# First entry's float32 attention scores on 64 rows of TensorE per head, with the first weight chunks issued by ScalarE

## The chip, the cores and the metric

One core of one Trainium2 chip runs the kernel. The metric is device microseconds of one execution. All times below are microseconds unless they are marked ns. The engines are called PE (TensorE, matrix products), DVE (VectorE), ACT (ScalarE), POOL (GpSimd) and SP (SyncE, which does no arithmetic here and issues transfers).

## The reference

Block-causal attention, followed by two feed-forward networks, all in float32:

```python
scores = scale * np.matmul(q, k.transpose(0, 1, 3, 2))      # (4, 8, 576, 576), head size 64
scores = np.where(block_i >= block_j, scores, -1000000000.0) # blocks of 64 positions
attn = softmax(scores); x = np.matmul(attn, v)               # x becomes (2304, 512)
h = np.maximum(np.maximum(x @ w1, x @ w2), x @ w3)           # d_ff 768
x = h @ w_out
h = np.maximum(x @ w_in, 0.0)                                # d_ff 2048
out = h * h @ w_out2
```

The scores of q and k are large enough that the kernel computes them in float32 or in a split form of it. The weights arrive as 8-byte numbers and are turned into a high and a low float32r part on the chip.

## The kernel before, in words

The batch has 4 entries; an entry has 8 heads, taken as 4 pairs, so there are 16 pairs. A pair's 576 query positions are cut into a first group of 256 (steps 0 and 1, of 128 each) and a second of 320 (steps 2 and 3, and a last step of 64). A step computes scores (tiles `sc`, in PSUM), masks a 64-wide corner, takes the row maximum (`nm`), exponentiates on ACT (`P`, with row sums `sm`), transposes P on PE (`tp`), copies it to SBUF (`ta`, `tb`) and, once per group, multiplies with v (`av`), scales by the reciprocal sums spread over rows (`r`, `rs`) and splits the result into `xh` and `xl`.

The first entry (pairs 0 to 3) takes its scores directly in float32. `score_operands_f32` (L486) loads three tiles: k of both heads on 128 partitions, and for each head a copy of q in which the other head's 64 partitions hold zeros. So each product contracts over 128 partitions, half of which add zero. In steps 0 and 1 the two heads' scores stand side by side in one PSUM bank, and one memset and one reduce serve both. The later entries split q and k into high and low parts and are not touched by the change, except that a small tile `zt` comes from an array of its own.

The weights of the first feed-forward network come in 24 chunks: 18 of `w1` (6 columns c, 3 matrices i, named `raw_w_c_i`) and 6 of `wo1`. A chunk is a transfer of 512 KB, two passes of ACT (128x512 each), two operations of DVE, an integer addition on POOL, a cast on ACT (`w1h`) and a subtraction on DVE (`w1l`). `with_weights` (L751) hands out the next chunk while it walks through the attention of the first entry: 0.7 chunks per step in the first groups of all four pairs, then 1.5 chunks per step in the second groups. The products `l` of the first feed-forward network (`mlp1`) need `xh`, `xl`, `w1h` and `w1l`; they share the PSUM banks with tag `mlp` with some of the score tiles, and come behind those.

The order on each engine isn't the order in which the program writes the operations. `Plan` collects them with their dependences and `Plan.issue` puts them out one by one: always the operation that by its own estimate can start first, on ties the one with the lower rank and then the one noted first. `duration` and `transfer` hold its prices. What it has put out each engine executes strictly in that order, so an instruction that waits holds up all behind it.

Eight completion semaphores are shared by the transfers in turn, so a transfer issued while eight are out waits until the oldest has landed.

Of the kernel before, what the change touches and what calls it, by code (L numbers as in the profile page):

```python
# [12 lines left out]
F32 = mybir.dt.float32  # L13
# [30 lines left out]

CFG = dict(PD=-1, PE=1, A1=0, A2=0, WP=1, FC=(8, 16), WO=55, FI=0, LO2=0, HI2=0, Q2=0, RN=3, XL=2, HL=2, SO=0, TF=0, W_A=0.7, W_B=1.5, SPARE='hl..rhl..rhl..r..r..r', S=15, PB=3, QB=(2, 2, 3), BANKS=(3, 2, 1, 2), LO=0, HI=0, Q=0, EV=('*', '*'), EV2=('a', 'a'), CB=2, PC=0, PM=1000, PX=-0.5, PO=0, HH='*', XH='*', N0='a', YS='a', HIS=0, RB=1, TB=(2, 1), KB=1, CT='a', LT='d', XA=4, XB=0)
W_A, W_B = CFG["W_A"], CFG["W_B"]
SPARE = CFG["SPARE"]
BANKS = dict(zip(("sc", "tp", "av", "mlp"), CFG["BANKS"]))

S_F32 = [CFG["S"] >> n & 1 for n in range(PAIRS)]  # L50
PB = CFG["PB"]
# [117 lines left out]
class Plan:  # L169
# [56 lines left out]
    def issue(self):  # L226
# [21 lines left out]
        for _ in ops:  # L248
            best = None
            for e, w in waiting.items():  # L250
                if not w:
                    continue
                other = held["pool" if e == "dve" else "dve"] if e in held else 0.0
                start = {i: max(free[e], at, other if port else 0.0) for i, (at, port) in w.items()}
                t = min(start.values())
                i = min((i for i, s in start.items() if s <= t), key=lambda i: (ops[i].rank, i))
                if best is None or t < best[0]:
                    best = t, e, i
            t, e, i = best
            op = ops[i]  # L260
            op.engine = e
            length = duration(e, op) * SLOW[e]
            if e in held and waiting[e][i][1]:
                held[e] = t + length - HOLD[e]
            for other in op.engines:
                del waiting[other][i]
            if e == "sp":
                queue = max(t + 1500, queue) + transfer(op)
                op.end, free[e] = queue + 400, t + 60
            else:  # L270
                op.end = t + length
# [41 lines left out]
def duration(engine, op):  # L313
# [3 lines left out]
    if engine == "pe":  # L317
        stat, mov = op.args[1:] if op.args[1:] else (op.kw["lhsT"], op.kw["rhs"])
        if op.name == "transpose":
            return 109  # L320
        n, m = width(op.args[0]), width(stat)
        if stat.tile.args[1] == F32:
            return (4 * n / 2.4 + 5) * (0.5 if m == 64 else 1)
        return max(n, 230) / 2.4 + (11 if n < 300 else 13)
# [17 lines left out]
def transfer(op):  # L342
    x = next(v for v in op.views())
    return 128 * 4 * width(x) / 320.0


@with_exitstack
def fused_kernel(ctx: ExitStack, tc: tile.TileContext, z0, k0, qk, v, w123, wo1, win2, wo2, out):
    nc = Plan(tc)
    mm = nc.tensor.matmul  # L350

# [6 lines left out]
    warm = const.tile([128, 1], F32, name="warm")  # L358
    tc.nc.vector.memset(warm, 0.0)
    tc.nc.scalar.activation(out=warm, in_=warm, func=AF.Exp)  # L360
    make_identity(tc.nc, ident.tile.real)
# [8 lines left out]
    at = Pool(nc, es_a.enter_context(tc.tile_pool(name="at", bufs=1, side="right", reuse_waits="tile")))  # L370
    ps = Pool(nc, ctx.enter_context(tc.tile_pool(name="ps", bufs=1, space=PSUM)), psum=True)

    def bank(name, tag):
# [7 lines left out]
    def load_w_(src, hi, lo, name, f=None):  # L381
# [8 lines left out]
        else:  # L390
            raw = m1.tile([128, 512, 2], U32, tag="wraw", bufs=2, name=f"raw_{name}")
            if f is None:
                f = m1.tile([128, 512], F32, tag="wf", bufs=2, name=f"f_{name}")
        nc.sync.dma_start(out=raw, in_=src.bitcast(U32).rearrange("p (n t) -> p n t", t=2))
        low, high = raw[:, :, 0], raw[:, :, 1]
# [59 lines left out]
    def score_operands(n):  # L455
# [18 lines left out]
        nc.sync.dma_start(out=kt, in_=k0[n])  # L474
        nc.sync.dma_start(out=zt, in_=z0[n, :, :, TAIL:])
        if CFG["TF"]:
# [9 lines left out]
    def score_operands_f32(n, g):  # L486


        a, w = GROUPS[g] if n < NPAIR else (0, S)
        if n < NPAIR and g == 0:  # L490
            zk = at.tile([128, 3, GA], F32, tag="tb", bufs=2 * CFG["TB"][1], name=f"zk{n}")
            z, k = [zk[:, h] for h in range(2)], zk[:, 2]
        else:
            z = [at.tile([128, w], F32, tag=t, bufs=CFG["QB"][2 * (t == "kl")], name=f"z{n}_{t}") for t in ("qs", "kl")]
            k = at.tile([128, S], F32, tag="kh", bufs=CFG["QB"][1], name=f"k{n}")
        nc.sync.dma_start(out=z[0], in_=z0[n, :, 0, a:a + w])
        nc.sync.dma_start(out=k, in_=k0[n, :, :a + w])
        nc.sync.dma_start(out=z[1], in_=z0[n, :, 1, a:a + w])
        return [[(z[h], k)] for h in range(2)], None

# [16 lines left out]
    def prefetch(n, g):  # L517


        f32 = bool(n < NPAIR and g == 0 or S_F32[n])  # L520
        with nc.ranked(CFG["PO"]):
            ops[n] = f32, score_operands_f32(n, g) if f32 else score_operands(n), value_operands(n, g)

    def attn_pair(n, groups=(0, 1)):
# [29 lines left out]
        def step(i):  # L554
# [3 lines left out]
            share = i < 2  # L558
            sc = [bank(f"sc{name}_{h}", sc_tag(i)) for h in range(1 if share else 2)]
            P = [at.tile([128, 576], F32, tag="P", bufs=PB, name=f"P{name}_{h}") for h in range(len(sc))]  # L560
            if share:
                both = sc[0][:, :2 * N].rearrange("p (h k) -> p h k", h=2)
                sc = [both[:, h] for h in range(2)]
                P = [P[0][:, N * h:N * h + N] for h in range(2)]
            nm = small(f"nm{name}")
            scale = SCALE if sf else 1.0
            sm = sums[i // 2][:, 2 * (i % 2):2 * (i % 2) + 2] if direct else small(f"sm{name}")
            for h in range(2):
                for c, (qp, kp) in enumerate(score[h]):
                    mm(sc[h][:, :N], qp[:, 128 * i - q0:128 * i - q0 + 128], kp[:, :N], start=c == 0,  # L570
                       stop=c == len(score[h]) - 1)
                if not share:
                    nc.vector.memset(sc[h][0:64, N - 64:N], MASKED / scale)
                    nc.vector.tensor_reduce(out=nm[:, h:h + 1], in_=sc[h][:, :N], axis=AX.X, op=ALU.max, negate=True)
            if share:
                nc.vector.memset(both[0:64, :, N - 64:N], MASKED / scale)
                nc.vector.tensor_reduce(out=nm, in_=both, axis=AX.X, op=ALU.max, negate=True)
# [173 lines left out]
    def with_weights(steps, per_step):  # L751
        due = 0.0
        for _ in steps:
            due += per_step
            while due >= 1:
                due -= 1
                f = next(weights, None)
                if f:
                    f()

    with_weights(attention(0, groups=(0,)), W_A)
    with_weights(attention(0, groups=(1,)), W_B)
# [286 lines left out]
```

## Time and profile before

| | us |
|---|---|
| runs | 884.64, 886.14, 887.04 (median 886.14) |
| the profiled execution | 888.7 |
| its span from first to last instruction | 886.9 |
| PE busy | 864.2 (97%) |
| DVE busy | 601.1 (68%) |
| ACT busy | 424.9 (48%) |
| POOL busy | 104.0 (12%) |

The profiled execution is longer than its span by 1.8, and 2.56 above the median of the runs. Shares over the whole span hide that the first 108 us are another kernel than the rest: there the weights are split and attention runs on ACT and DVE, and the transfers are dense. The trace is therefore read by stretches. All of the kernel's own operations carry one line, that of the helper which calls the engine (L187 before, L185 after), so groups are told apart by tile names.

### The profile page before, as it was taken

The numbers are of one execution on the slowest core, as the hardware profiler recorded it, in microseconds if no ns is written. First come the engines' busy times: TensorE is split into PE (matmuls) and PEld (weight loads), VectorE is DVE, ScalarE is ACT, GpSimd is POOL, SyncE is SP. The second block draws the span as 40 slices with busy tenths as digits, with TensorE's granted clock in tenths as the row PEclk, the third lists the DMA queues.
The fourth block names the chain that finished last, engine by engine and source line by source line (L and its number), as shares of the span: only waits on it lengthen the run. The fifth ranks groups of instructions, "written<-read, shape, count | busy, mean of one in ns | idle before, by whom it ended". The sixth has DMA issues, their size and how long they took to land.

```text
span 886.9 us, 14852 instructions
## 1 busy us (share of the span) xinstructions
PE 864.2 (97%) x5464; PEld 777.7 (88%) x5464; DVE 601.1 (68%) x1376; ACT 424.9 (48%) x1016; POOL 104.0 (12%) x94
## 2 busy tenths in 40 slices
PE   5899999999999999999999989999999999999997
PEld 4567799998999989899999979898999989999896
DVE  6998678878788988646557766546755457544543
ACT  6888667667688787544555231113211114211111
POOL 2233200000001111214442230000000000000000
PEclk9999999999999999999999999999999999999999
DMA  8745432232255563554656578454765536655221
GB/s 294 237 138 174 131 114 89 85 115 86 85 184 177 175 213 118 196 190 165 257 203 237 164 299 338 160 230 168 270 229 184 207 145 229 215 200 196 72 72 71
DMA packets 52056, 157.73 MB, mean 178 GB/s; under 512 B 8592, under 2 KB 16016, under 8 KB 48400
## 3 DMA queue, kind: packets, MB, share of 16 engines
q1 hardware_dynamic: 51984, 156.78, 50.5%
q8 instruction: 43, 0.70, 0.3%
q14 instruction: 29, 0.24, 0.1%
HBM read 124.26 MB, written 32.51 MB: 177 GB/s over the span
## 4 chain that ended last, share of the span: by engine, by line
PE 92%; DVE 2%; DMA 2%; ACT 2%; issue 0%; POOL 0%; SPq 0%; ACTq 0%; POOLq 0%; DVEq 0%
PE l L187 34%; PE acc L187 22%; PE ph_x L187 11%; PE ph_y L187 8%; PE av L187 5%; PE sc L187 5%; PE tp L187 4%; PE sc_t L187 2%; DMA raw_wi<-in_win 1%; PE tp_t L187 1%; DMA raw_wo<-in_wo 1%; DMA zk<-in_k 1%; PE r L187 0%; ACT P L187 0%; DVE f_wo L187 0%
## 5 line engine op out<-in xcount | busy, mean ns | idle before, releaser
L187 PE MATMUL acc<-woh,g 128*128 128x512 f32 x576 | 198.5, 395 | 0.0
L187 PE MATMUL l<-xh,w1l 128*128 128x256 f32 (+1 forms) x576 | 174.3, 303 | 0.9 <-DVE run L187 0.9
L187 PE MATMUL l<-xl,w1h 128*128 128x256 f32 (+1 forms) x576 | 172.2, 299 | 0.0
L187 PE MATMUL l<-xh,w1h 128*128 128x256 f32 (+1 forms) x576 | 172.2, 299 | 0.0
L187 ACT CAST g<-c 128x384 fp32r<-128x384 f32 x96 | 49.3, 513 | 220.8 <-DVE c L187 220.8
L187 PEld LDWEIGHTS acc<-woh,g 128*128 128x128 f32 x576 | 108.5, 189 | 19.4
L187 PE MATMUL acc<-wol,g 128*128 128x512 f32 x288 | 113.3, 393 | 0.0
L187 PEld LDWEIGHTS l<-xh,w1l 128*128 128x128 f32 x576 | 109.0, 189 | 4.1 <-issue 1.5
L187 PEld LDWEIGHTS l<-xl,w1h 128*128 128x128 f32 x576 | 109.1, 189 | 2.6 <-issue 1.7
L187 PEld LDWEIGHTS l<-xh,w1h 128*128 128x128 f32 x576 | 109.1, 189 | 1.9 <-issue 1.2
L187 PE MATMUL ph_x<-t,wq 128*128 128x384 f32 x432 | 87.7, 337 | 2.7 <-ACT p L187 2.7
L187 PEld LDWEIGHTS ph_x<-t,wq 128*128 128x128 f32 x432 | 77.4, 188 | 8.9 <-ACT p L187 3.1
L187 DVE TENSOR_TENSOR g<-c,g 128x384 fp32r<-128x384 f32 x96 | 53.6, 560 | 43.0 <-ACT g L187 42.6
L187 ACT ACTIVATE P<-sc,nm 128x128 f32<-128x128 f32 (+3 forms) x128 | 66.9, 530 | 9.9 <-DVE nm L187 8.4
L187 DVE TENSOR_TENSOR run<-l,run 128x256 f32<-128x256 f32 (+1 forms) x96 | 43.7, 455 | 27.9 <-PE l L187 26.3
L187 POOL TENSOR_TENSOR f_wo<-f_wo,raw_wo 128x512 int32<-128x512 int32 x22 | 29.8, 1357 | 276.5 <-DVE sm L187 180.3
L187 PEld LDWEIGHTS acc<-wol,g 128*128 128x128 f32 x288 | 54.3, 189 | 7.8
L187 PE MATMUL l<-hh,wo1l 128*128 128x256 f32 (+1 forms) x192 | 57.7, 306 | 2.2 <-DVE wo1l L187 2.1
L187 PE MATMUL ph_y<-b,wq 128*128 128x384 f32 x288 | 58.3, 337 | 0.0
L187 PE MATMUL l<-hl,wo1h 128*128 128x256 f32 (+1 forms) x192 | 57.5, 301 | 0.0
L187 PE MATMUL l<-hh,wo1h 128*128 128x256 f32 (+1 forms) x192 | 57.4, 300 | 0.0
L187 DVE TENSOR_REDUCE nm<-sc 128x2 f32<-128x256 f32 (+2 forms) x96 | 55.1, 588 | 0.8
(135 smaller groups left out, 1613.1 us busy)
## 6 DMA issues: line engine op xcount, KB each, us to landing
wq<-wq_d SPq DMA_DIRECT2D x20, 1792.0 KB, 8.6
wq_d<-wq SPq DMA_DIRECT2D x8, 1792.0 KB, 7.7
raw<-in_qk SPq DMA_DIRECT2D x24, 576.0 KB, 3.8
wol<-wo_d SPq DMA_DIRECT2D x48, 256.0 KB, 3.2
woh<-wo_d SPq DMA_DIRECT2D x48, 256.0 KB, 4.8
raw_wo<-in_wo SPq DMA_DIRECT2D x22, 512.0 KB, 3.8
raw_w<-in_w SPq DMA_DIRECT2D x18, 512.0 KB, 5.0
wo_d<-wos SPq DMA_DIRECT2D x16, 512.0 KB, 3.1
```

Of the source, the lines that this page charges most:

```text
L187: return getattr(engine, op_name)(*map(value, args), **{k: value(x) for k, x in kw.items()})
```

## The change

It does these things:

- `kernel`: the host lays out, for the first entry, q and k of a pair side by side (`qf0` for the first group, 256 + 256 columns; `qf1` for the second, 320 + 576), each head on its own 64 partitions, without zeros. `zt0` holds the zero-padded last 64 queries that the later entries use.
- `score_operands_f32`: one transfer fills one tile `f` in place of three transfers. Head h uses partitions 64h to 64h + 63 of it, so a score product contracts over 64 rows of TensorE.
- `step`: in the first entry's steps 0 and 1 each head gets a bank, a memset and a reduce of its own.
- `load_w_`: the first four chunks (`DA=4`) are issued by ACT instead of SP, and they are noted before the attention, not in turn with it. The rest are handed out at 0.7 and 1.5 per step as before, so 9 chunks instead of 5 are noted by the end of the first groups.
- The warming activation (with its table load) becomes a planned operation behind these issues.
- The planner prices a transfer 1.4 times longer where it is issued before 6 us, any issue at 430 ns of its engine, and a float32 product on a 64-row tile `f` at half.

```diff
-CFG = dict(PD=-1, PE=1, A1=0, A2=0, WP=1, FC=(8, 16), WO=55, ...
+CFG = dict(PD=-1, PE=1, A1=0, A2=0, WP=1, DA=4, WO=55, ...
...
-            if e == "sp":
-                queue = max(t + 1500, queue) + transfer(op)
-                op.end, free[e] = queue + 400, t + 60
+            if op.name == "dma_start":
+                queue = max(t + 1500, queue) + transfer(op) * (1.4 if t < 6000 else 1)
+                op.end, free[e] = queue + 400, t + 430
...
-            return (4 * n / 2.4 + 5) * (0.5 if m == 64 else 1)
+            return (4 * n / 2.4 + 5) * (0.5 if m == 64 or stat.area.shape[0] == 64 and stat.tile.kw["name"][0] == "f" else 1)
...
-        nc.sync.dma_start(out=raw, in_=src.bitcast(U32).rearrange("p (n t) -> p n t", t=2))
+        (nc.scalar if len(chunks) <= CFG["DA"] else nc.sync).dma_start(out=raw, in_=src.bitcast(U32).rearrange("p (n t) -> p n t", t=2))
...
-        a, w = GROUPS[g] if n < NPAIR else (0, S)
-        if n < NPAIR and g == 0:
-            zk = at.tile([128, 3, GA], F32, tag="tb", bufs=2 * CFG["TB"][1], name=f"zk{n}")
-            z, k = [zk[:, h] for h in range(2)], zk[:, 2]
-        else:
-            z = [at.tile([128, w], F32, tag=t, bufs=CFG["QB"][2 * (t == "kl")], name=f"z{n}_{t}") for t in ("qs", "kl")]
-            k = at.tile([128, S], F32, tag="kh", bufs=CFG["QB"][1], name=f"k{n}")
-        nc.sync.dma_start(out=z[0], in_=z0[n, :, 0, a:a + w])
-        nc.sync.dma_start(out=k, in_=k0[n, :, :a + w])
-        nc.sync.dma_start(out=z[1], in_=z0[n, :, 1, a:a + w])
-        return [[(z[h], k)] for h in range(2)], None
+        a, w = GROUPS[g]
+        t = at.tile([128, w + a + w], F32, tag=("tb", "qs")[g], bufs=(2 * CFG["TB"][1], CFG["QB"][0])[g], name=f"f{n}_{g}")
+        nc.sync.dma_start(out=t, in_=qf[g][n])
+        t = [t[64 * h:64 * h + 64] for h in range(2)]
+        return [[(x[:, :w], x[:, w:])] for x in t], None
...
+            one = share and not sf
+            sc = [bank(f"sc{name}_{h}", sc_tag(i)) for h in range(1 if one else 2)]
...
+    for _ in range(CFG["DA"]):
+        next(weights)()
+
+    nc.scalar.activation(out=warm, in_=warm, func=AF.Exp)
     with_weights(attention(0, groups=(0,)), W_A)
     with_weights(attention(0, groups=(1,)), W_B)
```

How the planner's order moves is shown at three places. In names such as `P_0_0_401` the first two numbers are step and head or half, the last is a counter of the program.

ACT at the start, of the change; the chunks `raw_w_0_0` and `raw_w_0_1`, and the first exponentials `P` of pair 0:

```order
L185 DMA raw_w_0_0_80<-in_w 128x1024
L185 DMA raw_w_0_1_84<-in_w 128x1024
L185 DMA raw_w_0_2_88<-in_w 128x1024
L185 DMA raw_w_1_0_92<-in_w 128x1024
L185 ACT_TABLE_LOAD
L185 ACTIVATE warm<-warm 128x1
L185 ACTIVATE raw_w_0_0_80<-raw_w_0_0_80 128x512 x2
L185 CAST w1h_132<-raw_w_0_0_80 128x512
L185 ACTIVATE raw_w_0_1_84<-raw_w_0_1_84 128x512 x2
L185 ACTIVATE P_0_0_143,sm_0_144<-sc_0_0_111,nm_0_122 128x128
```

Before, ACT's first exponentials stood behind one pass of one chunk; now they stand behind both passes and the cast of the first chunk and both passes of the second.

ACT around the first exponential of pair 3, the last pair of the first groups (`P_0_0_329` before, `P_0_0_401` in the change). Before, ending with it:

```order
L187 ACTIVATE raw_w_1_1_100<-raw_w_1_1_100 128x512
L187 CAST k2h_270<-kt_116 128x576
L187 CAST z2h_272<-zt_118 128x128
L187 CAST w1h_275<-f_w_1_0_249 128x512
L187 ACTIVATE P_0_0_305,sm_0_306<-sc_0_0_279,nm_0_294 128x128 x2
L187 ACTIVATE P_1_0_314,sm_0_306<-sc_1_0_281,nm_1_297 128x256 x2
L187 ACTIVATE P_0_0_329,sm_0_330<-sc_0_0_288,nm_0_309 128x128 x2
```

and in the change:

```order
L185 ACTIVATE P_1_0_334,sm_0_305<-sc_1_1_274,nm_1_291 128x256
L185 ACTIVATE raw_w_2_1_177<-raw_w_2_1_177 128x512
L185 ACTIVATE f_w_3_0_354<-raw_w_3_0_212 128x512
L185 ACTIVATE raw_w_3_0_212<-raw_w_3_0_212 128x512
L185 CAST w1h_365<-raw_w_2_0_170 128x512
L185 ACTIVATE f_w_2_2_368<-raw_w_2_2_235 128x512
L185 ACTIVATE raw_w_2_2_235<-raw_w_2_2_235 128x512
L185 ACTIVATE raw_w_3_1_337<-raw_w_3_1_337 128x512
L185 CAST w1h_365<-f_w_2_1_324 128x512
L185 ACTIVATE P_0_0_401,sm_0_402<-sc_0_0_328,nm_0_349 128x128
```

Ahead of this exponential stood 10 passes and 4 casts of weight chunks; now it is 21 passes and 8 casts. The exponentials of pairs 0 to 2 and the copies of their results stand ahead of it in both.

PE where the first products `l` of the feed-forward network stand. Before:

```order
L187 MATMUL sc_2_1_322<-k_104,z_kl 128x384
L187 MATMUL tp_1_0_334<-ident,P_1_0_314 128x128 x4
L187 MATMUL l_0_0_0_0_342<-xh_0_215,w1l_202 128x256
L187 MATMUL l_0_0_0_0_342<-xl_0_223,w1h_188 128x256
```

and in the change:

```order
L185 MATMUL sc_2_0_360<-f_1_99 128x384
L185 MATMUL av_0_370<-ta_319,v_0_191 64x256 x2
L185 MATMUL av_0_370<-ta_319,v_0_191 64x128 x2
L185 MATMUL r_0_397<-ident,sm_0_305 64x128 x4
L185 MATMUL tp_0_0_410<-ident,P_0_0_401 128x128
L185 MATMUL l_0_0_0_0_414<-xh_0_244,w1l_137 128x256
L185 MATMUL l_0_0_0_0_414<-xl_0_251,w1h_132 128x256
```

Before, the first `l` stood behind the transposes of pair 2; now it stands behind the first transpose of pair 3. The products `sc_2_0` and `sc_2_1` of the two heads are not next to each other in either.

## Rows read from the trace of the kernel before

**Rows 1.** The page, chain of work that ended last, by engine.

```profile
PE 92%; DVE 2%; DMA 2%; ACT 2%; issue 0%; POOL 0%; SPq 0%; ACTq 0%; POOLq 0%; DVEq 0%
```

**Rows 2.** Busy time by stretches: length, each engine's busy time, clock, DMA share, GB/s.

```profile
0.00:27.30 27.30, 16.42 (x87) 11.42 (x87) 18.42 (x51) 17.65 (x51) 6.23 (x11) 1.00 0.90 301
27.30:48.00 20.70, 19.43 (x147) 13.10 (x144) 20.29 (x54) 19.32 (x51) 8.10 (x6) 1.00 0.69 225
48.00:96.00 48.00, 48.00 (x349) 36.77 (x345) 39.79 (x97) 42.38 (x100) 17.02 (x13) 1.00 0.43 138
96.00:108.00 12.00, 9.83 (x80) 7.96 (x79) 9.49 (x19) 8.44 (x20) 2.85 (x2) 0.98 0.41 140
```

**Rows 3.** Timeline of PE: start, duration, operation, [idle before]; the first product l.

```profile
27.29 0.36 PE L187 MATMUL l<-xh,w1l 128*128 128x256 f32 x1
```

**Rows 4.** Waits of PE from 0 to 120 us: total, times, longest.

```profile
PE l L187 <- DVE wo1l L187: 2.1, 2, 1.7
```

**Rows 5.** Timeline of ACT, from the first weight pass to pair 3's exponential.

```profile
7.57 0.66 ACT L187 ACTIVATE raw_w<-raw_w 128x512 f32<-128x512 f32 x1 [5.35 <-DMA raw_w<-in_w]
...
18.46 0.69 ACT L187 ACTIVATE f_w<-raw_w 128x512 f32<-128x512 f32 x1
19.03 0.68 ACT L187 ACTIVATE raw_w<-raw_w 128x512 int32<-128x512 uint32 x1
...
20.39 0.65 ACT L187 CAST w1h<-f_w 128x512 fp32r<-128x512 f32 x1
20.91 0.72 ACT L187 ACTIVATE raw_w<-raw_w 128x512 int32<-128x512 uint32 x1
...
25.26 0.37 ACT L187 ACTIVATE P<-sc,nm 128x128 f32<-128x128 f32 x1 [2.25 <-DVE nm L187]
...
26.85 0.38 ACT L187 ACTIVATE P<-sc,nm 128x128 f32<-128x128 f32 x1
```

**Rows 6.** Timeline of DVE and POOL: the other operations of the first chunk.

```profile
8.27 0.43 DVE L187 TENSOR_SCALAR raw_w<-raw_w 128x512 int32<-128x512 int32 x1 [0.67 <-ACT raw_w L187]
8.73 0.69 DVE L187 SCALAR_TENSOR_TENSOR raw_w<-raw_w 128x512 int32<-128x512 int32 x1
...
10.47 1.29 POOL L187 TENSOR_TENSOR raw_w<-raw_w 128x512 int32<-128x512 int32 x1 [9.17 <-ACT raw_w L187]
```

**Rows 7.** Chain of work that ended last, in order of time: start, length, what.

```profile
12.34 0.66 PE r L187 x8
13.00 0.90 PE av L187 x8
...
26.45 0.65 PE sc L187 x2
...
92.43 0.44 PE tp L187 x4
```

**Rows 8.** Timeline of PE around products of the last steps (64 output rows each).

```profile
33.92 0.41 PE L187 MATMUL sc_t<-k,z_qs 128*64 128x288 f32 x1
...
34.16 0.41 PE L187 MATMUL sc_t<-k,z_qs 128*64 128x288 f32 x1
...
49.47 0.70 PE L187 MATMUL sc_t<-k,z_qs 128*64 128x288 f32 x2
50.10 0.55 PE L187 MATMUL tp<-ident,P 128*128 128x128 f32 x3
50.58 0.70 PE L187 MATMUL sc_t<-k,z_kl 128*64 128x288 f32 x2
51.21 0.39 PE L187 MATMUL l<-xl,w1h 128*128 128x256 f32 x1
```

**Rows 9.** DVE's groups on scores from 0 to 48 us: busy, mean ns.

```profile
L187 DVE TENSOR_REDUCE nm<-sc 128x2 f32<-128x512 f32 x4 | 2.7, 683 | 0.0
...
L187 DVE TENSOR_REDUCE nm<-sc 128x2 f32<-128x256 f32 x4 | 1.6, 396 | 0.0
...
L187 DVE MEMSET sc<- 64x64 f32 x7 | 0.8, 112 | 0.0
```

More of the change, by code (lines that the diff above doesn't have):

```diff
@@ L43 @@
 PAIRS = B * NPAIR
-CFG = dict(PD=-1, PE=1, A1=0, A2=0, WP=1, FC=(8, 16), WO=55, FI=0, LO2=0, HI2=0, Q2=0, RN=3, XL=2, HL=2, SO=0, TF=0, W_A=0.7, W_B=1.5, SPARE='hl..rhl..rhl..r..r..r', S=15, PB=3, QB=(2, 2, 3), BANKS=(3, 2, 1, 2), LO=0, HI=0, Q=0, EV=('*', '*'), EV2=('a', 'a'), CB=2, PC=0, PM=1000, PX=-0.5, PO=0, HH='*', XH='*', N0='a', YS='a', HIS=0, RB=1, TB=(2, 1), KB=1, CT='a', LT='d', XA=4, XB=0)
+CFG = dict(PD=-1, PE=1, A1=0, A2=0, WP=1, DA=4, WO=55, FI=0, LO2=0, HI2=0, Q2=0, RN=3, XL=2, HL=2, SO=0, TF=0, W_A=0.7, W_B=1.5, SPARE='hl..rhl..rhl..r..r..r', S=15, PB=3, QB=(2, 2, 3), BANKS=(3, 2, 1, 2), LO=0, HI=0, Q=0, EV=('*', '*'), EV2=('a', 'a'), CB=2, PC=0, PM=1000, PX=-0.5, PO=0, HH='*', XH='*', N0='a', YS='a', HIS=0, RB=1, TB=(2, 1), KB=1, CT='a', LT='d', XA=4, XB=0)
 W_A, W_B = CFG["W_A"], CFG["W_B"]
@@ L48 @@
 BANKS = dict(zip(("sc", "tp", "av", "mlp"), CFG["BANKS"]))
-S_F32 = [CFG["S"] >> n & 1 for n in range(PAIRS)]
 PB = CFG["PB"]
@@ L347, in fused_kernel @@
 @with_exitstack
-def fused_kernel(ctx: ExitStack, tc: tile.TileContext, z0, k0, qk, v, w123, wo1, win2, wo2, out):
+def fused_kernel(ctx: ExitStack, tc: tile.TileContext, qf0, qf1, zt0, k0, qk, v, w123, wo1, win2, wo2, out):
     nc = Plan(tc)
+    qf = qf0, qf1
     mm = nc.tensor.matmul
@@ L358, in fused_kernel @@
     warm = const.tile([128, 1], F32, name="warm")
-    tc.nc.vector.memset(warm, 0.0)
-    tc.nc.scalar.activation(out=warm, in_=warm, func=AF.Exp)
     make_identity(tc.nc, ident.tile.real)
@@ L371, in fused_kernel @@
     ps = Pool(nc, ctx.enter_context(tc.tile_pool(name="ps", bufs=1, space=PSUM)), psum=True)
+    warm = Pool(nc, const).tile([128, 1], F32, name="warm")
+    nc.vector.memset(warm, 0.0)
     def bank(name, tag):
@@ L474, in score_operands @@
         nc.sync.dma_start(out=kt, in_=k0[n])
-        nc.sync.dma_start(out=zt, in_=z0[n, :, :, TAIL:])
+        nc.sync.dma_start(out=zt, in_=zt0[n])
         if CFG["TF"]:
@@ L517, in prefetch @@
     def prefetch(n, g):
-        f32 = bool(n < NPAIR and g == 0 or S_F32[n])
+        f32 = n < NPAIR
         with nc.ranked(CFG["PO"]):
@@ L558, in step @@
             share = i < 2
-            sc = [bank(f"sc{name}_{h}", sc_tag(i)) for h in range(1 if share else 2)]
-            P = [at.tile([128, 576], F32, tag="P", bufs=PB, name=f"P{name}_{h}") for h in range(len(sc))]
-            if share:
+            one = share and not sf
+            sc = [bank(f"sc{name}_{h}", sc_tag(i)) for h in range(1 if one else 2)]
+            P = [at.tile([128, 576], F32, tag="P", bufs=PB, name=f"P{name}_{h}") for h in range(1 if share else 2)]
+            if one:
                 both = sc[0][:, :2 * N].rearrange("p (h k) -> p h k", h=2)
                 sc = [both[:, h] for h in range(2)]
+            if share:
                 P = [P[0][:, N * h:N * h + N] for h in range(2)]
@@ L571, in step @@
                        stop=c == len(score[h]) - 1)
-                if not share:
+                if not one:
                     nc.vector.memset(sc[h][0:64, N - 64:N], MASKED / scale)
                     nc.vector.tensor_reduce(out=nm[:, h:h + 1], in_=sc[h][:, :N], axis=AX.X, op=ALU.max, negate=True)
-            if share:
+            if one:
                 nc.vector.memset(both[0:64, :, N - 64:N], MASKED / scale)
@@ L1017 @@
     qn, kn = [a.reshape(PAIRS, 2, D, S) for a in (q.transpose(0, 1, 3, 2), k.transpose(0, 1, 3, 2))]
-    z0 = np.zeros((PAIRS, 2, D, 2, S), q.dtype)
+    zt0 = np.zeros((PAIRS, 2, D, 2, S - TAIL), q.dtype)
     for h in range(2):
-        z0[:, h, :, h] = qn[:, h]
-    z0, k0 = z0.reshape(PAIRS, 128, 2, S), kn.reshape(PAIRS, 128, S)
+        zt0[:, h, :, h] = qn[:, h, :, TAIL:]
+    zt0, q0, k0 = zt0.reshape(PAIRS, 128, 2, S - TAIL), qn.reshape(PAIRS, 128, S), kn.reshape(PAIRS, 128, S)
+    qf = [np.concatenate([q0[:NPAIR, :, a:a + w], k0[:NPAIR, :, :a + w]], axis=2) for a, w in GROUPS]
     qk = np.stack([a.transpose(0, 2, 1, 3) for a in (qn, kn)], axis=3)
@@ L1037 @@
     arrays = {
-        "z0": z0, "k0": k0, "qk": qk, "v": vc, "w123": w123, "wo1": w["moe_w_out"], "win2": win2, "wo2": w["moe2_w_out"],
+        "qf0": qf[0], "qf1": qf[1], "zt0": zt0, "k0": k0, "qk": qk, "v": vc, "w123": w123, "wo1": w["moe_w_out"], "win2": win2, "wo2": w["moe2_w_out"],
     }
```

## The prediction, on record before the changed kernel ran

> **What bounds the kernel now.** I read the chain of waits first: PE carries 92% of it [rows 1]. So the time is PE's work plus the time in which PE stands, and the question is where it stands. The table of stretches [rows 2] answers that for the first entry. Up to 27.30 PE is busy for 16.42, so it stands for 10.88. From there to 48 it stands for 1.27, from 48 to 96 not at all, and from 96 to 108 for 2.17. The timeline gives the border its meaning: at 27.29 the first product l of the feed-forward network starts [rows 3], and from then on PE has two kinds of work to mix. The stop after 96 is a wait for a split weight chunk, `wo1l` on DVE [rows 4]. Hence two levers: what comes ahead of the first l, and how much work PE has behind it. The other engines matter as far as they set that start. ACT and DVE are busy for 19.32 and 20.29 of the 20.70 behind it, so whatever is put ahead in their queues pushes back what it passes [rows 2].
>
> **What ACT must do before the first l.** This is the term that decides. In the new order the first l stands on PE behind the first transpose of pair 3, and that waits for pair 3's first exponential. Ahead of that exponential stand 21 weight passes and 8 casts, where there were 10 and 4; everything else ahead of it is the same. A pass costs 0.57 from start to start (18.46 to 19.03), a cast 0.52 (20.39 to 20.91) [rows 5]. So ACT has 11 x 0.57 + 4 x 0.52 = 8.4 more to do first.
>
> Against that stands an earlier start. The first chunk's first pass began at 7.57, when the chunk had landed [rows 5]; SP issued it behind four other transfers. Now it is ACT's first instruction. It shares the DMA engines with the operands of pair 0, which SP issues at the same moment: 0.52 MB and 0.26 MB at the 301 GB/s of this stretch [rows 2] take 2.6, with issue and landing on top. I take 6.0, nearer to the row, since the transfers are as dense as before; so 1.6 is gained. The bounds are 7.57, no gain, and 3.5 (its own bytes in 1.7 and as much again for issue and landing), which puts 4.1 ahead.
>
> Then ACT's own waits. It stood for 2.25 before 25.26, waiting for a row maximum [rows 5]. In the new order a cast follows the first two passes, and needs two DVE operations and a POOL addition: 0.43, 0.69 and 1.29 [rows 6], begun after one pass, so ACT waits about 0.43 + 0.69 + 1.29 + 0.57 for the pass less the 1.14 of the two passes, which is 1.8, or 2.0 with the gaps between engines. The one wait replaces the other: 0, between -2 (more weights fill the gap at 25.26, and the cast's chain overlaps) and +2 (both happen).
>
> Together pair 3's exponential comes 8.4 - 1.6 + 0 = 6.8 later, at 33.7 instead of 26.85 [rows 5]. Before, l did not wait for it; now it does, and an exponential with its transpose takes about 0.7 (0.57 and some 0.1 for a transpose). The first l moves from 27.29 to 34.4, by 7.1. With the bounds: 2.6 to 10.7. On PE one more `av` and `r` group and one less `sc` product stand ahead of it, 0.90 + 0.66 - 0.65 of work [rows 7] that is done in the waiting time: -0.9.
>
> **What comes back later.** The weights are now ahead of the attention, so part of the later standing should go. There are 1.27 + 2.17 = 3.4 to be had [rows 2], in the second of which PE waits for just such a chunk [rows 4]. I take half, -1.7, with 0 and -3.4 as bounds.
>
> **64 rows.** In steps 0 and 1 the two heads' products are mostly neighbours in the new order and use different halves of the array. What they save by overlapping lies ahead of the first l, where PE stands for 10.88 anyway [rows 2], so it is worth 0; if that cover were gone it would be at most half of those products. In steps 2 and 3 the heads' products stand far apart, so they have nothing to overlap with and stream as many columns as before: 0.
>
> The cost of changing the shape of the array does show. A last step's products use half of the columns. In the trace three transposes, then such a pair, then an l take 50.10 to 51.21, that is 1.11 [rows 8]. Three transposes at 0.11 each [rows 7] and two products at 0.24 from start to start (33.92 to 34.16) [rows 8] would be 0.81, so going there and back costs 0.3. The new order has 31 such excursions from the full array before the second entry, the old one 22. I take 9 x 0.3 = +2.7, between 0 (half the rows need no such stop) and +3.9 (26 more changes of shape, at 0.15 each). The Trainium skill ("TensorEngine Tiling (Array Packing)", section Key Properties) says that changing the tiling mode drains TensorE, which speaks against this change; the trace agrees for half the columns with 0.3 per excursion, and no row shows it for half the rows. By that rule the term would be the upper bound, +3.9, and the sum 1.2 higher.
>
> One of the eight last-step couples was torn apart before, at 49.47 and 50.58, 0.63 each until the next product starts [rows 8]. In the new order both heads of each couple are neighbours: -0.6.
>
> **DVE, transfers, issues.** Each pair of the first groups gets two reduces of 128 and two of 256 columns for one of 256 (0.396) and one of 512 (0.683) [rows 9]. None of the new ones is wider than the 256 at 0.396, so at most 1.58 for 1.08. Two more memsets at 0.112 [rows 9] make it at most 0.7 per pair, 2.9 in all. ACT's queue is the longer one by the sum above, so I take 0, and +2.9 as the upper bound, since DVE has 20.29 of 20.70 to do right behind [rows 2]. Without the zeros 1.2 MB fewer are moved, nearly 4 us at 301 GB/s, and 16 issues on SP. Neither is on the path as I see it: pair 3 waits behind work on ACT, not for its operands. What covers that is ACT's queue of weight passes; without it the operands would be what is late. The four issues fall before ACT has anything to do: it stood for 5.35 ahead of its first pass [rows 5]. The skill ("DMA: Bandwidth & Descriptors", section Issuing engines are not separate DMA queues) has it that a second issuing engine saves only issue time; by that the chunks' earlier arrival is taken from the operands, and nothing of the 1.6 would be a gain in bytes.
>
> **The sum.** +7.1 - 0.9 - 1.7 + 2.7 - 0.6 = +6.6; the low ends give 2.6 - 0.9 - 3.4 + 0 - 0.6 = -2.3, the high ends 10.7 - 0.9 + 0 + 3.9 - 0.6 + 2.9 = +16.0. Against the profiled execution that is 888.7 + 6.6 = 895.3. That execution is 2.56 above the median of the runs, so for a median I say 886.14 + 6.6, rounded to 892.7. A measurement of this kernel can tell about 0.3%, 2.7 us, from no change.
>
> **The rivals.**
> *The splitting of weights is the bound, and it starts earlier: faster.* If the stretch to 108 ends when the last chunk is split, then what counts is that ACT and DVE begin up to 4.1 earlier (first landing at 3.5 instead of 7.57), and the end moves with them: 882.0. For it: PE's stop after 96 is a wait for `wo1l` [rows 4], and ACT is busy for 42.38 of the 48 before it. Against it: PE has no gap from 48 to 96 [rows 2], so it carries that stretch itself, and a later begin of l cannot be made good there. It decides if the first l starts before about 28.
> *The shift and what comes back cancel: no change.* First chunk at 4.5, only the cast's wait: 8.4 - 3.1 - 2 = +3.3 for the exponential, +3.6 for l; then -0.9 - 3.4 + 1.5 - 0.6 gives +0.2: 886.3. For it: the low ends are each possible. Against it: they must come together.
> *DVE is the longer queue, and every change of shape drains: much slower.* 10.7 - 0.9 - 1.0 + 3.9 + 2.9 - 0.6 = +15: 901. For it: DVE's share behind 27.30. Against: ahead of 27.30 DVE has 8.9 to spare.
> *The heads on 64 rows don't overlap at all.* Then PE's work ahead of the first l stays what it was, and what covered it before covers it still: the forecast's time, and I count it there.
>
> **How the numbers follow.** My forecast gets 0.48 (889 to 898), much slower 0.10, no change 0.22, faster 0.20. Slower by over 0.3% is the first two, 0.58. Its own range is 889 to 898. The range for 8 in 10 reaches to the faster case's 882 and to 899; what lies below and above gets 0.1 each.
>
> **What would show it.** Right: the first l at 32 to 36; ACT's exponentials of pair 3 behind 21 passes, with a wait of about 2 before the first cast; PE's standing before the first l up by 5 or more and the waits for `wo1l` after 96 gone or halved; products of 64 rows with about 0.3 lost around each that stands alone, and neighbours that overlap in steps 0 and 1. Wrong: a first l before 30, or gaps on PE before it that do not grow. Then ACT's queue was not what pair 3 waits for. If the gaps grow and the time doesn't, the later stop gave back more than the 3.4 that I can see.

## The result, and the profile after

The change made the kernel slower. Its four runs are 894.04, 894.87, 897.06 and 900.49 us, median 895.96, beside 886.59 for the kernel before in runs on the same chip: a ratio of 1.0112 (of the means), with a 95% interval from 1.0065 to 1.0159. The forecast was 892.7, between 882 and 899, with 0.58 for slower. The profiled execution of the changed kernel took 894.0, with a span of 892.3. That of before had 888.7, over its own median, so two profiles differ by less than two medians do.

The first product l, which the forecast put at 34.4 instead of 27.29 [rows 3], starts later still. In the timeline of PE after the change (start, duration, operation, idle before):

```profile
4.89 1.66 PE L185 MATMUL sc<-f 64*128 64x128 f32 x8 [4.89 <-DMA f<-in_qf]
10.60 1.40 PE L185 MATMUL tp<-ident,P 128*128 128x128 f32 x4 [4.05 <-ACT P L185]
...
14.89 1.55 PE L185 MATMUL av<-ta,v 128*64 128x256 f32 x8 [0.78 <-DVE ta L185]
...
38.62 0.56 PE L185 MATMUL l<-xh,w1l 128*128 128x256 f32 x1
```

PE gets its first operands at 4.89 (3.51 before), and then stands for exponentials. The table of waits of PE after the change (total, times, longest) says the same; `wo1l`, for which it stood before [rows 4], is not in it any more:

```profile
PE tp L185 <- ACT P L185: 10.9, 7, 4.1
PE sc L185 <- DMA f<-in_qf: 4.9, 1, 4.9
```

Behind that start PE is nearly always busy. The table of stretches after the change (length, then busy time of PE, PEld, DVE, ACT and POOL, the granted clock, the transfers' share and rate), over the stretches of [rows 2]:

```profile
0.00:27.30 27.30, 13.27 (x56) 7.06 (x58) 15.88 (x52) 16.54 (x41) 7.78 (x11) 1.00 0.82 299
27.30:48.00 20.70, 18.34 (x99) 10.85 (x97) 17.31 (x53) 17.36 (x47) 9.47 (x7) 0.84 0.53 160
48.00:96.00 48.00, 46.13 (x317) 32.50 (x316) 38.00 (x93) 38.02 (x91) 12.79 (x11) 1.00 0.43 139
96.00:108.00 12.00, 12.00 (x84) 7.67 (x83) 8.34 (x22) 7.98 (x22) 3.48 (x3) 1.00 0.26 74
```

Up to 96 PE is busy for 13.27 + 18.34 + 46.13 = 77.74 where it was 83.85, so it stands 6.1 longer; 2.17 come back up to 108. The granted clock is a row that the forecast did not have: 0.84 from 27.3 to 48, where the kernel before has 1.00 [rows 2].

To follow the loss through the program I take one product that every kernel of this study computes: the 49th product `l<-hh,wo1l` of 256 columns, in the second half of the attention's stretch. Ahead of it PE executes the same products in all of them, if not always in the same order (2656 records, and the 80 dummies that e4, e5 and e8 add). In the timeline of PE of the kernel before, and then of the changed one, it is:

```profile
373.93 0.28 PE L187 MATMUL l<-hh,wo1l 128*128 128x256 f32 x1
```

```profile
382.85 0.28 PE L185 MATMUL l<-hh,wo1l 128*128 128x256 f32 x1
```

The delay at this marker is 8.9, close to the 9.4 between the medians. Thus the loss is made ahead of it; of the 11.3 at the first l, 2.4 net are given back. Behind it the two profiles come closer again, to 5.4 between their spans, chiefly since the kernel before has a stop at the start of the second network that the changed one does not have:

```profile
519.52 1.50 PE L187 MATMUL ph_x<-t,wq 128*128 128x384 f32 x6 [2.70 <-ACT p L187]
```

The profiled execution of before lies over its median, so how much of this a typical execution gives back is not shown.

What ACT did between its first pass and pair 3's first exponential stands in its groups of that stretch (operation, shapes, count, then busy time, mean ns, and idle time before):

```profile
L185 ACT ACTIVATE raw_w<-raw_w 128x512 int32<-128x512 uint32 x10 | 6.7, 665 | 0.0
L185 ACT ACTIVATE f_w<-raw_w 128x512 f32<-128x512 f32 x6 | 4.0, 673 | 0.0
L185 ACT ACTIVATE raw_w<-raw_w 128x512 f32<-128x512 f32 x5 | 3.3, 669 | 0.6 <-DMA raw_w<-in_w 0.6
...
L185 ACT CAST w1h<-raw_w 128x512 fp32r<-128x512 f32 x4 | 2.4, 610 | 2.1 <-POOL raw_w L185 2.1
...
L185 ACT CAST w1h<-f_w 128x512 fp32r<-128x512 f32 x4 | 2.4, 617 | 0.9 <-POOL f_w L185 0.9
```

These are the 21 passes and 8 casts. In the timeline of ACT after the change the places where it waits are:

```profile
5.07 1.22 ACT L185 ACTIVATE raw_w<-raw_w 128x512 f32<-128x512 f32 x2 [0.55 <-DMA raw_w<-in_w]
8.37 0.62 ACT L185 CAST w1h<-raw_w 128x512 fp32r<-128x512 f32 x1 [2.08 <-POOL raw_w L185]
...
19.44 0.37 ACT L185 ACTIVATE P<-sc,nm 128x128 f32<-128x128 f32 x1 [2.68 <-DVE nm L185]
...
25.90 0.59 ACT L185 COPY ta<-tp 128x512 f32<-128x512 f32 x1 [1.76 <-PE tp L185]
...
37.60 0.36 ACT L185 ACTIVATE P<-sc,nm 128x128 f32<-128x128 f32 x1
```

From 5.07 to 37.60 ACT is busy for 24.33 and stands for 8.20; before, from 7.57 to 26.85 [rows 5], for 15.71 and 3.57. So pair 3's exponential is 10.75 later: 8.6 of work, 4.6 of standing, less 2.5 for the earlier start. What the wait of 2.68 was for stands in DVE's timeline after the change:

```profile
17.39 0.49 DVE L185 TENSOR_REDUCE nm<-sc 128x1 f32<-128x128 f32 x2
...
18.64 0.69 DVE L185 SCALAR_TENSOR_TENSOR f_w<-raw_w,f_w 128x512 int32<-128x512 int32 x1
19.25 0.16 DVE L185 TENSOR_SCALAR nm<-nm 128x2 f32<-128x2 f32 x1
```

The two separate reduces take 0.49. The maximum's scaling comes 1.4 behind them, since work on a weight chunk stands between them in DVE's queue.

### The profile page after: what moved, and what is told of

It is laid out like the page before. It is cut to its first block, busy times and chain, and to the rows that moved or that the text cites. A ratio compares the mean times of both kernels' runs of the same rounds, so it can differ in the third digit from the quotient of the medians.

```text
span 892.3 us, 14834 instructions
## 1 busy us (share of the span) xinstructions
PE 868.9 (97%) x5464; PEld 773.2 (87%) x5464; DVE 604.0 (68%) x1396; ACT 421.6 (47%) x1012; POOL 103.7 (12%) x94
## 4 chain that ended last, share of the span: by engine, by line
PE 96%; ACT 2%; DVE 1%; DMA 0%; issue 0%; POOL 0%; DVEq 0%; ACTq 0%
PE l L185 35%; PE acc L185 22%; PE ph_x L185 11%; PE ph_y L185 8%; PE sc L185 6%; PE av L185 6%; PE tp L185 4%; PE sc_t L185 2%; PE tp_t L185 1%; PE r L185 1%; DMA raw_w<-in_w 0%; ACT raw_w L185 0%; ACT w1h L185 0%; ACT P L185 0%; DVE raw_w L185 0%
## 5 line engine op out<-in xcount | busy, mean ns | idle before, releaser
L185 PE MATMUL tp<-ident,P 128*128 128x128 f32 x320 | 53.3, 284 | 10.9 <-ACT P L185 10.9
L185 DVE SCALAR_TENSOR_TENSOR c<-c 128x384 f32<-128x384 f32 x96 | 56.1, 587 | 1.9
```

Of the source, the lines that this page charges most:

```text
L185: return getattr(engine, op_name)(*map(value, args), **{k: value(x) for k, x in kw.items()})
```

## The experiments

Theory A is the forecast's main term: ACT's queue of weight passes. Its rival, theory B, is that the products on 64 rows cost by themselves. Theory D came when the granted clock had been seen; theory E, that each 64-row product among full-height ones costs a few tenths for the change of shape, came from the trace of e6. Times are medians, and the ratios are of means; each group of experiments shares its runs of the kernel before (885.3, 885.8 and 886.2). The delay is that of the marker above, from one profile each. How far two executions differ there shows in the change and its repetition, 8.9 and 9.7. At the first l they differ more: e9, whose edit stands behind the first l, has it at 28.68 for 27.29.

| kernel | us | ratio to before, 95% interval | first l | delay at the marker |
|---|---|---|---|---|
| change, again | 895.07 | 1.0113 (1.0096 to 1.0130) | 39.23 | 9.7 |
| e1, 64 rows, no first chunks on ACT | 903.79 | 1.0216 (1.0192 to 1.0240) | 35.53 | 17.8 |
| e2, first chunks on ACT, 128 rows | 891.28 | 1.0072 (1.0052 to 1.0093) | 37.99 | 4.5 |
| e3, change with fewer chunks ahead | 905.50 | 1.0229 (1.0209 to 1.0249) | 32.47 | 15.7 |
| e4, change and dummies | 897.33 | 1.0132 (1.0097 to 1.0166) | 39.05 | 11.2 |
| e5, e1 and dummies | 911.99 | 1.0296 (1.0268 to 1.0324) | 36.39 | 24.0 |
| e6, before, second groups on 64 rows | 892.20 | 1.0078 (1.0047 to 1.0110) | 28.94 | 4.6 |
| e8, before and dummies | 896.18 | 1.0103 (1.0062 to 1.0144) | 31.46 | 6.8 |
| e9, before, last products on 64 rows | 885.75 | 0.9998 (0.9980 to 1.0015) | 28.68 | -0.4 |
| e10, change, second groups on 128 rows | 895.23 | 1.0114 (1.0075 to 1.0154) | 39.86 | 4.2 |
| e11, e10 without first chunks on ACT | 892.76 | 1.0081 (1.0048 to 1.0113) | 34.70 | 5.0 |
| e12, change, heads together | 894.65 | 1.0088 (1.0060 to 1.0117) | 38.78 | 1.6 |

### One part at a time

The first four kernels are the change again and three variants. The edits:

```diff
e1:  -CFG = dict(... WP=1, DA=4, ...
     +CFG = dict(... WP=1, DA=0, ...
e2:  the kernel before, with the change's lines on DA, on the planner's
     price of transfers and on the warming activation
e3:  -CFG = dict(... W_A=0.7, ...
     +CFG = dict(... W_A=0.2, ...
```

Expected of the change again:

> The changed kernel once more, beside the others on their chip. Every theory: about 9 us over the kernel before (ratio 1.011), between +5 and +14.

of e1:

> The change without its four early chunks (DA=0): all chunks issued by SyncE and noted in turn; 64 rows per head and one operand transfer stay. Ahead of pair 3's first exponential ScalarE then has 11 weight passes instead of 21 (10 before). Theory A (the chunks put ahead hold up pair 3 on ScalarE): the first product l starts at 26 to 31 us and the time is within 3 us of the kernel before (-2 to +3, the upper end if each stop for a change of the array's shape shows). Theory B (the 64-row products are what costs: shape changes and their drains): first l early too, but the time stays 5 or more above the kernel before.

of e2:

> The kernel before with only the early chunks: four issued by ScalarE and noted ahead, the planner's new transfer prices; scores on 128 rows with zeros in three transfers. 20 weight passes stand ahead of pair 3's first exponential. Theory A: first l at 34 to 39 us, time +5 to +10 over the kernel before. Theory B: within 2 us of the kernel before.

of e3:

> The change with 0.2 instead of 0.7 chunks per step handed out in the first groups: ScalarE still issues four chunks at the start and they stay first in its queue, but 13 passes instead of 21 stand ahead of pair 3's first exponential. Theory A: first l at 28 to 32 us, time 0 to +4 over the kernel before, so 5 or more below the change. Theory B: as the change, +7 to +11. A third theory C (it is the issue by ScalarE and its place at the start, not the number of passes): as the change.

The repetition is within 0.9 us of the first measurement. The chunks alone cost 5.9, as A says. But e1, with hardly a longer queue on ACT than before (11 passes and 5 casts ahead of pair 3 for 10 and 4), is slower by 18, and e3, in which ACT's queue is shorter than in the change (13 and 5), is slower than the change by 10. A alone falls; so does B alone, by which e2 should have been within 2 of the kernel before. e1 and e3 have a first l ahead of the change's, and lose the time behind it. The timeline of PE in e1 shows where:

```profile
27.84 0.47 PE L185 MATMUL tp<-ident,P 128*128 128x128 f32 x1 [5.58 <-ACT P L185]
...
36.90 1.65 PE L185 MATMUL sc<-f 64*128 64x384 f32 x2
38.47 1.55 PE L185 MATMUL av<-ta,v 128*64 128x256 f32 x8
...
45.94 0.37 PE L185 MATMUL l<-xl,w1h 128*128 128x256 f32 x1
46.15 0.28 PE L185 MATMUL l<-xh,w1h 128*128 128x256 f32 x1
46.36 0.87 PE L185 MATMUL av<-ta,v 128*64 128x256 f32 x8
```

The same eight `av` products take 1.55 at 38.47 and 0.87 at 46.36. The table of stretches of e1 gives the clock beside it:

```profile
28.00:36.00 8.00, 8.00 (x24) 3.97 (x25) 5.00 (x19) 3.25 (x14) 0.41 (x1) 0.50 0.29 104
36.00:44.00 8.00, 8.00 (x25) 4.15 (x25) 2.75 (x8) 5.06 (x13) 1.66 (x2) 0.50 0.15 44
```

After a wait of 5.58 PE was busy without a stop, and the granted clock was 0.50 of full speed, the level of 1.2 GHz, till about 46. That is 18 us of work at half speed, by estimate some 9 us lost. In the change the lower level is there too (an `av` of 1.55 at 14.89). PE stands for exponentials in that stretch, so most of the loss should be covered; this is argued here, and the next runs were to test it.

### Keeping PE busy with dummies, and the second groups alone

Theory D then says that the lower clock is what the change costs beyond A. e4, e5 and e8 put ten transposes of the identity ahead of the first real one of steps 0 and 1 of four pairs, into the same bank, where they are overwritten. e6 is the kernel before with its zeros and transfers, in which the second groups' products read only the 64 rows that are not zero; the order of instructions stays that of before.

```diff
e4, e5, e8 (on the change, on e1, on before):
+            for _ in range(CFG["DUM"] if hasattr(op, "pre") else 0):
+                self.tc.keep_in_program_order(self.call(self.real[e], "transpose", op.pre, {}))
...
+                    if share and direct and h == 0 and j == 0:
+                        op.pre = t[:, 256:384], ident, ident
e6:
+        if g == 1:
+            return [[(z[h][64 * h:64 * h + 64], k[64 * h:64 * h + 64])] for h in range(2)], None
```

Expected of e4:

> The change, with ten transposes of the identity matrix (their result is overwritten) put on TensorE right ahead of the first real transpose of each of steps 0 and 1 of the first four pairs; everything else as in the change. Theory D (part of the change's loss is that TensorE runs at the lower of its two clock levels, av at 1.5 us and r at 1.1 instead of 0.88 and 0.66, because it stood too much of the time ahead of these products): av and r between 10 and 31 us are at 0.9 and 0.66, the granted clock between 32 and 42 us stays above 0.9, and the time falls by 2 to 5 us, to 890 to 893. Theory A (the queue of ScalarE's casts is the cause, the clock only follows its waits): the time stays within 1.5 us of the change's 895, or rises by the dummies' own time. If the clock rises and the time stays, the lower clock lay beside ScalarE's work and cost nothing.

of e5:

> The 64-row products without the extra chunks on ScalarE (the e1_rows_only kernel, 903.8 us), with the same ten dummy transposes ahead of steps 0 and 1 of the first four pairs. Theory D (its loss of 18 us is the granted clock of 0.57 between 24 and 48 us, in which TensorE was busy all the time): the clock there rises above 0.9 and the time falls by 8 us or more, to 896 or less. Theory A (the loss comes from weight chunks that are late around 108 to 132 us, whatever the clock): the time stays within 2 us of 903.8. If the clock there stays near 0.57, the dummies do not reach its cause and the run tells nothing on the price.

of e6:

> The kernel before, with only the score products of the second groups (steps 2, 3 and the last ones) on 64 rows; operands, transfers, banks and the order of all instructions are those of before, so that ScalarE's queue is not moved. Excursions alone (the prediction's 0.3 us for each product that stands alone among full-height ones): 16 of them at the most, +3 to +5 us, 888 to 890.5. Theory D (products on 64 rows among the others also let the granted clock fall between 24 and 48 us): the clock there is below 0.9 and the time is 893 or more. Nothing at all: within 1.5 us of before.

of e8:

> The kernel before with the same ten dummy transposes ahead of steps 0 and 1 of the first four pairs: a control for what the dummies cost or bring alone. They stand in TensorE's waits, which are 31% of its first 27 us here, and its products ran at the lower level only in the first 12 us: expected -1.5 to +1.5 us against before. A gain above 1.5 us would say that the clock of the first 12 us is on the path in the kernel before too; a loss above 1.5 us that the dummies themselves push the chain, and must be added to what e4 and e5 show.

The control e8 spoils the instrument: dummies alone cost 10 us by the medians, 6.4 between the two profiles. In these PE's busy time rises by 9.5, 80 dummies of 0.12, and its standing falls by only 3.1, although PE stood for 10.88 of its first 27.30 [rows 2], more than the 31% that the expectation has. The dummies stand right ahead of transposes for whose results others wait. In e5 the clock stays at 0.50 from 28 to 44, as in e1, so that run tells nothing of the price. In e4 the clock did come up: the `av` products take 0.82 at 25.97, and pair 3's exponential starts at 35.97 instead of 37.60. Then ten dummies stand for 2.3 ahead of the last transpose, and the first l is at 39.05. So ahead of pair 3 the lower clock is worth at most 1.6 in the change; whether that would reach the end this run cannot say. What it costs behind the first l no run separates.

e6 is the clean one, since its order is that of before. It costs 6.4 (4.2 to 9.7), and 4.6 at the marker. That lies between the two bands that were expected; the granted clock from 24 to 48 is 0.95, so theory D's sign is not there. Look at one of its 16 products of 384 or 512 columns in the timeline of PE, in the kernel before:

```profile
38.92 0.66 PE L187 MATMUL tp<-ident,P 128*128 128x128 f32 x4
39.41 0.81 PE L187 MATMUL sc<-k,z_qs 128*128 128x384 f32 x2
39.77 0.69 PE L187 MATMUL l<-xh,w1l 128*128 128x256 f32 x2
40.30 0.28 PE L187 MATMUL l<-xl,w1h 128*128 128x256 f32 x1
```

and in e6:

```profile
40.73 0.66 PE L187 MATMUL tp<-ident,P 128*128 128x128 f32 x4
41.32 0.91 PE L187 MATMUL sc<-k,z_qs 64*128 64x384 f32 x2
42.16 0.50 PE L187 MATMUL l<-xh,w1l 128*128 128x256 f32 x2
42.50 0.28 PE L187 MATMUL l<-xl,w1h 128*128 128x256 f32 x1
```

From the transposes to the product it is 0.49 before and 0.59 now, from the product to the second l 0.89 and 1.18: an excursion of 0.1 + 0.3 = 0.4. Where a product with half the columns follows, it is less. In the kernel before:

```profile
48.13 0.55 PE L187 MATMUL tp<-ident,P 128*128 128x128 f32 x3
48.52 1.02 PE L187 MATMUL sc<-k,z_kl 128*128 128x512 f32 x2
49.47 0.70 PE L187 MATMUL sc_t<-k,z_qs 128*64 128x288 f32 x2
```

and in e6:

```profile
50.85 0.55 PE L187 MATMUL tp<-ident,P 128*128 128x128 f32 x3
51.33 1.12 PE L187 MATMUL sc<-k,z_kl 64*128 64x512 f32 x2
52.38 0.70 PE L187 MATMUL sc_t<-k,z_qs 64*64 64x288 f32 x2
```

From the transposes to `sc_t` it is 1.34 and 1.53, so 0.2. Read like this through both timelines, the eight products ahead of an l cost 0.4 each, the three ahead of transposes 0.3, the four ahead of products with half the columns 0.2, and the first is hidden by a wait: together 4.9, or 0.3 on average. The Trainium skill ("TensorEngine Tiling (Array Packing)", section Key Properties) says that a change of the tiling mode drains TensorE. The trace agrees, and gives 0.2 to 0.4 per excursion for half the rows.

The 4.6 at the marker is not these 4.9 alone. In this execution the clock was low ahead of the first 64-row product, which stands at 26.48; the kernel before has 1.00 in this stretch:

```profile
20.00:24.00 4.00, 2.79 (x9) 2.47 (x10) 3.90 (x7) 3.61 (x8) 1.81 (x2) 0.50 0.77 227
```

That made PE some 1.4 late, and later waits took up part of both.

### Where an excursion costs, and what the groups are worth

If the change of shape is what costs, then the last products, whose output used half of the columns before already, must be free on 64 rows (e9), and heads that follow each other must share one excursion (e12). e10 and e11 separate the groups.

```diff
e9, on before:
-                        mm(sc[x][64 * h:64 * h + 64, :HALF], qp[:, TAIL - q0:S - q0], kp[:, ks], start=True, stop=True)
+                        mm(sc[x][64 * h:64 * h + 64, :HALF], qp[64 * h:64 * h + 64, TAIL - q0:S - q0],
+                           kp[64 * h:64 * h + 64, ks], start=True, stop=True)
e10, on the change: for g == 1 the three tiles and transfers of before
e11: e10 with DA=0
e12, on the change, in steps 2 and 3:
+                pair[0].mate, pair[1].done = pair[1], pair[0]
+                pair[0].deps |= pair[1].deps - {pair[0]}
...
+            for o in (op, op.mate) if hasattr(op, "mate") else () if hasattr(op, "done") else (op,):
```

Expected of e9:

> The kernel before, with only the last queries' products (sc_t, 128x64 before, 288 columns, 32 of them) on 64 rows, order and transfers unchanged. Theory E (a 64-row product costs the 0.4 us that e6's trace shows around each 384- and 512-column pair because TensorE changes its way of working there; sc_t's weights were 64 columns wide already, and the same stretch of e6, from the transposes ahead of sc_t to the ones behind, took 1.21 us against 1.22 before): no change, within 1.5 us of before. If a 64-row product costs its 0.3 to 0.4 us wherever it stands: 8 groups, +2.4 to +3.2 us or more.

of e10:

> The change, with the second groups' products (steps 2, 3, last) back on 128 rows with their zeros and three transfers, as before; first groups and first chunks as in the change. Theory E: the 16 places in steps 2 and 3 at 0.4 us go, 895.5 - 6.4 = 889; with what is left of the late start (e2_chunks_only: +5.9 over before) 888 to 892. If instead the change's loss is all ScalarE's queue: 894 or more. If the first groups' overlap on 64 rows pays what it saves in work (30 products of 128 columns and 4 of 256 at half): under 886.

of e11:

> The same, without the first chunks on ScalarE: only the first groups on 64 rows, their operands in one transfer, their heads in two banks. It asks where the +18 us of e1_rows_only stand. Theory E: 903.8 - 6.4 = 897, so that the first groups alone (their late exponentials, 5.6 us of waiting at 22 us, and the lower clock behind it) cost +11. If the 64-row products of steps 2 and 3 hold the clock low after that wait: the granted clock between 28 and 46 us is above 0.8 here, against 0.5 there, and the time under 892. Nothing from the first groups at all: 886.

of e12:

> The change, with the second head's product of steps 2 and 3 issued right behind the first head's, always. Theory E: 8 places in place of 16 at 0.4 us, -3.2, and the two heads' products overlap, 4 x 0.32 + 4 x 0.43 = -3.0: 889 to 890 against the change's 895.5. Theory against it: both banks must be free before the first head's product may start, so that steps 2 and 3 start later and the gain goes into waits for banks: 895 or more. If they do not overlap (starts 0.3 us or more apart): -3 alone, 892.

**e9** is the kernel before to the measurement's bound (-1.8 to +1.3): 64 rows are free where the shape was not the full array anyway.

**e10** missed its 889: as a whole it is no faster than the change, and its 895.23 is in the band of the rival by which the whole loss is ACT's queue (894 or more). Yet at the marker it is 4.2 behind the kernel before, where the change is 8.9 behind. The second groups' 4.7 are gone there, and then lost again in one place, as its timeline of PE shows:

```profile
398.97 0.31 PE L185 MATMUL l<-xh,w1h 128*128 128x320 f32 x1
403.10 0.42 PE L185 MATMUL l<-xh,w1l 128*128 128x320 f32 x1 [3.82 <-ACT run L185]
```

Its timeline of ACT tells what was late:

```profile
402.11 0.62 ACT L185 CAST wos<-f_wo 128x512 fp32r<-128x512 f32 x1 [3.45 <-DMA wo_d<-wos]
402.63 0.42 ACT L185 COPY run<-l 128x320 f32<-128x320 f32 x1
```

A cast of a later weight waited for a buffer that a write to memory had not yet left, and the copy for which PE waited stood in ACT's queue behind it. With the lower clock behind this stop (0.79 from 404 to 412) it costs 5.6: the delay is 4.1 ahead of it and 9.8 behind. The change does not have this stop. So the time of the profiled execution is explained, but the 889 was not reached.

**e11** shows the first groups by themselves: 5.0 at the marker, of which the lower clock is a part. It is 4 faster than the 897 that theory E gave it, and near the other band (under 892, with a clock above 0.8 from 28 to 46, which is 0.82 here and 0.50 in e1). The second groups, which are all that e1 adds to it, cost about 12 there. PE is busy from 28 to 34.6 at 0.50, as in e1; but the level comes back at about 34.6, where in e1 it stayed till 46.

**e12** does share the excursions. The trace counts a float32 product of this kind twice. In the timeline of PE of e12 both heads' products of 384 columns (x4) take hardly longer than one head's alone in the change (x2, 0.91 at 53.96):

```profile
55.29 0.92 PE L185 MATMUL sc<-f 64*128 64x384 f32 x4
```

PE's work falls from 868.9 to 860.3, and the delay at the marker from 8.9 to 1.6. The profiled execution took 889.58. But that is the fastest of its six, whose median of 894.65 misses the expected 889 to 890; its interval overlaps that of the change. What the other five executions lose is not in any profile. So neither e10 nor e12 shows in its median that the time returns when the excursions go; e6 and the markers carry that reading.

## Why the prediction was right, and where its terms were not

The measured 895.96 is 3.3 over the forecast and inside its own range of 889 to 898. But two of its terms were off by about 4 each and cancelled, which is luck; a third was short by 2.6, and that is most of what is left.

*The first l.* Mechanism right, size too small: 38.62, not 34.4, outside the 32 to 36 that were named, and 11.3 later for an upper bound of 10.7. Work and order were as said: 21 passes and 8 casts, 8.6 more of busy time for 8.4. The earlier start gave 2.5, not 1.6. What failed is "ACT's own waits: 0, between -2 and +2". It is +4.6. The wait of 2.08 before the first cast is there (2.0 was expected), but it does not take the place of the one for the row maximum; that one grew to 2.68, and a new one of 1.76, for transposes on PE, came behind it. At the last of these the lower clock has its part: in e4 it is 0.53.

*What comes back.* Underestimated by about as much. The prediction had 7.1 - 0.9 - 1.7 = 4.5 for the late start with all that it brings. e2, which has nothing else, shows 10.7 at the first l and 4.5 at the marker. So the two errors cancelled. The stops for `wo1l` went, as said.

*64 rows in steps 0 and 1.* 0 was right beside the first chunks: e10 and e2 are 4.2 and 4.5 behind at the marker. The overlap is there: the first scores take 1.66 at 4.89, and in the kernel before

```profile
3.51 2.90 PE L187 MATMUL sc<-zk 128*128 128x128 f32 x8 [3.51 <-DMA zk<-in_k]
```

The cover that the prediction named, PE's standing ahead of the first l, fits that it brings nothing. Without the chunks on ACT the first groups cost 5.0 (e11), by another order on ACT and by the lower clock on a stretch in which PE has no stop; no run separates these two.

*64 rows in steps 2 and 3.* This is the term that was mis-sized. The prediction counted 9 excursions more at 0.3, 2.7 with an upper bound of 3.9, and took 0.6 off for a couple that was torn apart. The price is right on average; the number is not. All 16 products stand alone among others, and each costs, also beside products with half the columns, where the number of excursions does not grow. In e6 they add up to 4.9 in the timeline and 4.6 at the marker (6.4 by the medians), in the change to 8.9 - 4.2 = 4.7 at the marker. The two parts that were run alone, 4.5 (e2) and 4.6 (e6), make 9.1 for the 8.9 of the change; by the medians 5.9 and 6.4 are more than its 9.4 to 9.7, within their intervals.

*DVE and transfers.* Of DVE's longer work only ACT's wait of 2.68 for a row maximum and some 2 us of PE's waits could come. In the first of these the separate reduces take 0.49, and DVE's work on weights stands behind them; no run changed the reduces alone. That the chunks take from the operands shows: the first operands land at 4.89 in the change and at 3.43 in e11, where SP's transfers are alone; before it was 3.51. PE stands in that stretch anyway.

*The rivals.* "The splitting of weights is the bound" falls: it began 2.5 earlier, and nothing came of it. "No change" fails at ACT's waits. "Much slower" was 5 too high: it has the changes of shape right, but DVE's queue did not become the bound. That the heads do not overlap at all is refuted by the 1.66 above. The one not thought of is the clock, which weighs most in e1, e3 and e5.

No kernel here beats the one before; e9 equals it.

## What to carry to other kernels

A product on half the rows costs 0.3 to 0.4 us more than one with zeros if full-height work stands on both sides of it (0.2 beside products with half the columns), and saves time on PE only where the other half's product follows at once (0.92 for both in e12); pricing it at half, as the planner of the change does, is right only there. Follow one fixed late product through all variants: it separates losses that a total of the runs adds up with an unrelated stop, as in e10. And before a wait is moved to the start of a kernel, ask at which clock the work behind it will run.

## What was unexpected of the hardware

The lower clock level lasts for different times. In e1 PE has no stop from 27.84 on and gets the full level back at 46 (it was at the lower one before the wait too: an `av` of 1.52 at 18.73), in e11 none from 26.90 on and has it at 34.6; in e8, after 27.18, at about 31. The first has products on 64 rows among the others all the time, the second only to 31, the third none. No run varied these alone, so the cause stays open.

The granted clock in the table of stretches is 1.00 up to its first change, even where durations say otherwise: in the change's first 27.3 us it stands at 1.00, with `av` products at 1.55, the duration that e1 has at 0.50. Durations of one repeated group are the safer reading there.

Dummy work on PE, in a stretch in which PE stands for 40% of the time, cost 6.4 of its 9.5 between the profiles and all of it by the medians (e8). It stood ahead of just those instructions that others wait for.
